# Talking-heads attention with a gated feed-forward on one core: value products in runs of two chunks, loads issued from ScalarE's queue, and a weight repack in three steps

## The chip, the core and the metric

The kernel runs on one core of a Trainium2 chip. Its engines are TensorE (PE in the profile; its weight loads are listed as PEld), VectorE (DVE), ScalarE (ACT), GpSimd (POOL) and SyncE (SP), each with its own stream of instructions that it works off in order, and they meet through semaphores. DMAs are issued here from SP's stream and from ACT's stream; in the profile the issuing instructions stand under SPq and ACTq. The metric is the device time of one execution in microseconds. Less is better.

## What is computed

Four batches, twelve heads, 448 positions and a head size of 64. Scores are mixed across heads before the softmax (`w_pre`) and the probabilities after it (`w_post`); the result, 1792 tokens of 768, goes through a gated feed-forward layer of width 1536. All of it in 32-bit floats.

```python
scores = (q @ k.T) / sqrt(64)                     # per batch and head, 448 x 448
scores = einsum('bhij,hg->bgij', scores, w_pre)   # heads mixed
attn   = exp(scores - max(scores)); attn = attn / (sum(attn) + 1e-9)
attn   = einsum('bhij,hg->bgij', attn, w_post)    # heads mixed again
x      = (attn @ v) as 1792 tokens x 768
out    = (sigmoid(x @ w_gate) * (x @ w_val)) @ w_out
```

The matrices `moe_w_gate`, `moe_w_val` and `moe_w_out` come as 64-bit floats in memory, 36 tiles of 128 x 768, and are narrowed to 32 bits on the chip.

## The kernel before

**Attention (`_attention`).** The queries of a batch are cut in blocks of 120, 120, 120 and 88 rows, sixteen blocks in all, and a block in groups of ten rows: 180 groups. A group is a slot of a software pipeline, and the loop at L434 walks the slots t. For each (block, head) two matmuls (`qk`, L163 and L164) make the scores in PSUM, and a copy (`keep`, L172 on ACT for odd heads, L174 on DVE for even ones) puts them into a staging tile `st`, of which there are two, used by alternate blocks. `regroup` (L198) is a DMA from `st` into a tile `T`, which turns ten rows of twelve heads into 120 partitions; it is issued from SP up to seven slots ahead, into one of five `T` buffers. `premix` (L203) multiplies `T` by `w_pre` into a PSUM tile `pm` (two buffers), `rowmax` (L210, DVE) takes the row maximum, `expo` (L219, ACT) the exponential, `scale` (L233, POOL) and `p_lo` (L248, DVE) split the scaled probabilities in two 16-bit halves `ph` and `pl`, `postmix` (L260, PE, tile `mx`, two buffers) mixes the heads again, and `mix` (L266, ACT) puts the result into one of two block tiles. In the first 13 and the last 16 groups the halves are left out and a 32-bit product is made instead. When a block is whole, `av` (L280) multiplies it by the values: six chunks c per block, each 8 matmuls that the trace counts as 16, spread over the slots in which the next block is worked on; after chunks 3 and 5 ACT copies the sums out (L288) and issues their store (L289).

In a slot of the loop PE is given, in this order, `qk` of a coming block, `premix(t+4)`, `av` if one is due, `postmix(t)`. DVE is given the copy of `qk`, then `rowmax(t+4)`, then the small sums and `p_lo(t+1)`. ACT is given its copy of `qk`, `mix(t-1)`, the jobs of the plan (the `av` copies among them) and `expo(t+4)`.

The inputs are loaded by `k_load` (L122, 18 tiles, four buffers in `raws`), `q_load` (L140, 15 tiles, two buffers) and `v_load` (L181, 12 tiles, three buffers), one load per slot at most, by the times set at L329 to L353; all are issued from SP, in SP's stream between the regroup DMAs.

**The feed-forward (`_Moe`).** Its products are made by a seven-product scheme on 2 x 2 quarters, in two pairs of batches, and every 32-bit operand is split in two parts, `hi` by a cast on ACT (`round`, L875) and `lo` by a subtraction on DVE (`rest`, L878), so that three matmuls stand for one (`gate`, L888, and `out_mm`, L899). Sums and differences of quarters are made on DVE (`tt`, L881), PSUM is copied out by ACT (`copy`, L905) and added up on DVE (`sum`, L908); L911 is the sigmoid and L914 the product with the gate. For the first pair each weight tile k is loaded as raw 64-bit words (`load_raw`, L839, SP, three buffers in `raws`), its upper half is made in place in two steps on ACT (`top`: L848 takes the fifth byte of each 8-byte word, sign-extended, into the word's upper 32 bits, L852 turns the bfloat16 in the word's last two bytes into a float16), `convert` (L857, DVE) merges the two 32-bit words, and `keep_w` (L861) stores the 32-bit tile for the second pair.

Which unit does which of these tasks when is decided before anything is issued, by a planner in Python (`order_tasks`) that goes through the tasks with the prices that each carries (`by_dve`, `by_act`, the `pe` entries) and with the room for tiles of each kind (`ROOM`, `KIND`). It starts some thirty slots before the last group, so the first weight tiles are repacked while attention still runs. `slot`, `between` and `run` then issue the tasks in the planned order. The matmuls of the feed-forward keep one fixed order; what the prices move is the order of the tasks on ACT, DVE and SP.

## Time and profile before

| | us |
|---|---|
| median of 3 runs | 1010.58 |
| lowest and highest | 1008.87, 1017.09 |
| the profiled execution | 1007.51 |
| its span, first to last instruction | 1005.6 |
| attention: up to the first matmul of the feed-forward at | 508.3 |
| the feed-forward's second pair and tail, from about 725 to | 1005.6 |

The profile is of one execution. In its views times count from the start of the span; PE and PEld overlap, since a weight load runs beside the matmul before it. Idle time of an engine is put down to what ended it last, and idle time of an engine that nobody waits for costs nothing. The chain of waits is followed backwards from the last instruction, so its shares say what the time hung on at each moment, and not how much would go if one step went.

### The profile page before, as it was taken

How to read it: one execution, taken by the hardware profiler on the slowest of the kernel's cores; microseconds unless marked ns; L12 is line 12 of the kernel's file. 1: busy time of each engine (PE TensorE's matmuls, PEld its weight loads, DVE VectorE, ACT ScalarE, POOL GpSimd, SP SyncE). 2: the span in 40 equal slices, each digit the busy share in tenths (PEclk: the TensorE clock that was granted, in tenths of full speed). 3: DMA queues.
4: the chain of work that ended last, by engine and by line, in shares of the span. 5: the costliest groups of instructions: out<-in, count | busy, mean ns of one | idle time of the engine just before them, and what ended most of it. 6: DMA issues, size and time to landing. Idle time of an engine off the chain costs nothing.

```text
span 1005.6 us, 17847 instructions
## 1 busy us (share of the span) xinstructions
PE 939.6 (93%) x6606; PEld 749.7 (75%) x6606; DVE 696.9 (69%) x1243; ACT 613.1 (61%) x1061; POOL 275.7 (27%) x354
## 2 busy tenths in 40 slices
PE   7889999899989999979789999999899999999998
PEld 2656676566766677656568888888699999999997
DVE  7556777578665667645468877788988766669882
ACT  3555667566665666667596888799455444446460
POOL 6246755478546864422210000000000000000000
PEclk8899999999999999999999999999899999999999
DMA  5666567665677665766825555778644321210002
GB/s 162 158 165 171 133 129 190 156 169 114 146 195 173 139 125 118 176 164 133 237 90 185 192 189 188 250 242 292 207 146 166 94 63 52 75 48 1 28 10 74
DMA packets 71333, 144.48 MB, mean 144 GB/s; under 512 B 18167, under 2 KB 49999, under 8 KB 71247
## 3 DMA queue, kind: packets, MB, share of 16 engines
q1 hardware_dynamic: 58024, 137.63, 50.0%
q10 hardware_dynamic: 13223, 5.70, 2.1%
q8 instruction: 53, 0.87, 0.3%
q14 instruction: 33, 0.27, 0.1%
HBM read 79.44 MB, written 25.17 MB: 104 GB/s over the span
## 4 chain that ended last, share of the span: by engine, by line
PE 63%; DMA 17%; ACT 11%; DVE 5%; issue 3%; SPq 1%; ACTq 0%; DVEq 0%
PE bank L888 18%; DMA T<-st 13%; PE bank L899 13%; PE pm L203 11%; PE mx L260 9%; PE av L280 6%; DMA raws<-in_w_dram 4%; ACT raws L852 4%; PE qk L163 3%; ACT m_GV L875 3%; PE qk L164 2%; ACT raws L848 2%; ACT m_FWTR L905 1%; DVE st L174 1%; DVE m_FWTR L881 1%
## 5 line engine op out<-in xcount | busy, mean ns | idle before, releaser
L888 PE MATMUL bank<-m_GV 128*128 128x448 f32 x1512 | 314.2, 368 | 10.8 <-ACT m_FWTR L905 5.2
L888 PEld LDWEIGHTS bank<-m_GV 128*128 128x128 f32 x1512 | 284.1, 189 | 40.0 <-ACT m_FWTR L905 7.8
L210 DVE TENSOR_SCALAR_CACHE_REDUCE junk<-pm 128x448 f16<-128x448 f32 x180 | 112.0, 622 | 132.5 <-PE pm L203 129.1
L203 PE MATMUL pm<-T,w 120*128 120x448 f32 x360 | 173.2, 563 | 28.7 <-DMA T<-st 19.8
L219 ACT ACTIVATE e<-pm,nm 128x448 f32<-128x448 f32 x180 | 114.3, 635 | 124.7 <-DVE junk L210 71.9
L878 DVE TENSOR_TENSOR m_GV<-m_FWTR,m_GV 128x768 fp32r<-128x768 f32 (+1 forms) x137 | 154.4, 1138 | 49.9 <-ACT m_GV L875 47.9
L875 ACT CAST m_GV<-m_FWTR 128x768 fp32r<-128x768 f32 (+1 forms) x137 | 134.9, 1001 | 56.7 <-DVE m_FWTR L881 28.3
L899 PE MATMUL bank<-m_GV 128*128 128x448 f32 x756 | 158.9, 371 | 6.5 <-ACT m_GV L875 3.9
L899 PEld LDWEIGHTS bank<-m_GV 128*128 128x128 f32 x756 | 143.8, 191 | 21.2 <-ACT m_GV L875 4.7
L233 POOL TENSOR_SCALAR ph<-e,ss 128x448 f16<-128x448 f32 x151 | 98.5, 660 | 156.4 <-ACT e L219 94.8
L260 PEld LDWEIGHTS <-ph 128*128 128x128 f16 x1208 | 91.6, 98 | 47.4 <-issue 38.7
L248 DVE SCALAR_TENSOR_TENSOR pl<-e,ss,ph 128x448 f16<-128x448 f32 x151 | 122.2, 809 | 4.1 <-POOL ph L233 3.8
L266 ACT ACTIVATE mix<-mx,fm 128x480 f32<-128x480 f32 x180 | 121.2, 673 | 2.5 <-PE mx L260 2.5
L280 PEld LDWEIGHTS av<-mix,v 128*64 128x64 f32 x1504 | 73.6, 138 | 59.1 <-issue 40.5
L260 PE MATMUL mx<-w2hi,pl 128*128 128x120 f16 x604 | 105.2, 217 | 9.5 <-DVE pl L248 9.5
L260 PE MATMUL mx<-w2hi,ph 128*128 128x120 f16 x604 | 106.3, 219 | 1.5 <-POOL qhh L149 0.6
L260 PE MATMUL mx<-w2lo,ph 128*128 128x120 f16 x604 | 105.3, 217 | 0.0
L203 PEld LDWEIGHTS pm<-T,w 120*128 120x128 f32 x360 | 66.4, 194 | 46.7 <-ACT mix L266 15.7
L280 PE MATMUL av<-mix,v 128*64 128x120 f32 (+1 forms) x1504 | 93.5, 268 | 0.0
L905 ACT COPY m_FWTR<-bank 128x448 f32<-128x448 f32 x96 | 52.8, 554 | 60.4 <-PE bank L888 45.4
L163 PE MATMUL qk<-kT,qhh 128*120 128x448 f32 (+1 forms) x180 | 80.1, 445 | 2.4 <-POOL qhh L149 1.9
L174 DVE COPY st<-qk 120x448 f32<-120x448 f32 (+1 forms) x92 | 56.3, 613 | 35.4 <-PE qk L164 14.6
(70 smaller groups left out, 1041.6 us busy)
## 6 DMA issues: line engine op xcount, KB each, us to landing
T<-st SPq DMA_DIRECT2D x180, 210.0 KB
raws<-in_w_dram SPq DMA_DIRECT2D x36, 767.6 KB
w<-m_FWTR SPq DMA_DIRECT2D x36, 384.0 KB
m_FWTR<-w SPq DMA_DIRECT2D x31, 384.0 KB
raws<-in_kd_dram SPq DMA_DIRECT2D x18, 448.0 KB
qd<-in_qd_dram SPq DMA_DIRECT2D x11, 720.0 KB
raws<-w SPq DMA_DIRECT2D x17, 384.0 KB
v<-in_vb_dram SPq DMA_DIRECT2D x12, 512.0 KB
```

The source lines that it names most:

```text
L163: nc.tensor.matmul(sc[:n, :S], lhsT=hh[:, h, :n], rhs=kt, start=True, stop=False)
L203: nc.tensor.matmul(ps[:, :S], lhsT=w1, rhs=t_t.pop(t), start=True, stop=True)
L210: nc.vector.tensor_scalar(junk, sc_t[t][:, :S], -SCALE, None, op0=ALU.mult, op1=ALU.min, accum_out=nm)
L219: nc.scalar.activation(out=e, in_=sc_t.pop(t)[:, :S], func=AF.Exp, bias=nm_t.pop(t), scale=SCALE, accum_out=ss)
L248: nc.vector.scalar_tensor_tensor(pl, e_t.pop(t), ss_t.pop(t), p_t[t][0], op0=ALU.mult, op1=ALU.subtract)
L260: nc.tensor.matmul(ps[:, jb, :], lhsT=a[:, JB[jb]:JB[jb] + 128], rhs=w, start=(i == 0), stop=(i == len(terms) - 1))
L266: nc.scalar.activation(out=mixes[bi % 2][:, :, :, r0:r0 + R], in_=mx_t.pop(t).rearrange("p j (g r) -> p j g r", r=R), func=AF.Copy, scale=fm)
L280: nc.tensor.matmul(av_t[bi][64 * i:64 * i + 64, c % 4, :n], lhsT=vt[b, u][:, h + i, jb, :], rhs=mixes[bi % 2][:, jb, 2 * c + i, :n], start ...
L875: self.nc.scalar.copy(self.f32(hi).bitcast(F32R), self.f32(f))
L878: self.nc.vector.tensor_tensor(self.f32(lo).bitcast(F32R), self.f32(f), self.f32(hi), op=ALU.subtract)
L888: self.nc.tensor.matmul(self.f32(bank), lhsT=w[a][:, k], rhs=x[b][:, k], start=self.START[i] and k == r == 0, stop=k == self.KH - 1 and r ...
L899: self.nc.tensor.matmul(self.f32(bank), lhsT=w[a][:, k], rhs=b[bb], start=self.START[i] and j == k == r == 0, stop=j == OUT_TILES - 1 and ...
```

## The change

Five things are changed.

1. `av` takes its chunks in twos: chunk c is placed at the slot of chunk c - c % 2, and the two follow each other on PE, after `postmix(t)` and not before it (`tail`).
2. In a slot `premix` and `rowmax` now come before `qk` and its copy.
3. `k_load`, `q_load` and `v_load` are issued from ACT's stream, and so is `load_raw` in slots more than seven before the end of attention (four of the 36 tiles); the others stay on SP.
4. `top` has three steps. ACT takes the fifth byte of each word into a dense tile `half` of 768 16-bit numbers, DVE turns these from bfloat16 into float16 in place, and ACT spreads them, as 16-bit integers times 65536, into the upper 32-bit words. There is one `half`, so a tile's third step comes before the next tile's first. `raws` grows from 4608 to 4992 elements, and the last `ROOM` has four tiles of kind T where it had five.
5. The planner's prices: a fixed 0.18 where 0.07 stood for an ACT task, 0.205 where 0.19 stood for a matmul, and 0.4 for the new step on DVE.

```diff
 I32 = mybir.dt.int32
+I16 = mybir.dt.int16
 I8 = mybir.dt.int8
...
         t = kld[len(kraw) % len(kld)]
-        nc.sync.dma_start(out=t, in_=kd[b, c])
+        nc.scalar.dma_start(out=t, in_=kd[b, c])
         kraw[b, c] = t
...
         t = qld.tile([128, H * QB], F32, tag="qd", name="qd")
-        nc.sync.dma_start(out=t[:, :H * n], in_=qd[b, :, H * i0:H * (i0 + n)])
+        nc.scalar.dma_start(out=t[:, :H * n], in_=qd[b, :, H * i0:H * (i0 + n)])
         qraw[bi] = t[:, :H * n].rearrange("p (h s) -> p h s", s=n)
...
         t = vst.tile([128, QUAD, 4, D], F32, tag="v", name="v")
-        nc.sync.dma_start(out=t.rearrange("p h j d -> p (h j d)"), in_=vb[b, u])
+        nc.scalar.dma_start(out=t.rearrange("p h j d -> p (h j d)"), in_=vb[b, u])
         vt[b, u] = t
...
         for c in range(KC):
-            at(spread(c, KC, s0, s1), av, bi, c)
+            at(spread(c - c % 2, KC, s0, s1), av, bi, c)
             if bi == NBK - 1:
...
         todo = plan.get(t, ())
+        if 0 <= t + SOFT < NG:
+            premix(t + SOFT)
+            rowmax(t + SOFT)
         for fn, args in todo:
...
                 fn(*args)
-        if 0 <= t + SOFT < NG:
-            premix(t + SOFT)
-            rowmax(t + SOFT)
         sums = t % 2 == 0 and 0 <= t + PREP < NG + 1
...
             mix(t - 1)
+        tail = (av, moe.between)
         for fn, args in todo:
-            if fn is not qk:
+            if fn is not qk and fn not in tail:
                 fn(*args)
...
             expo(t + SOFT)
+        if t >= NG:
+            for fn, args in todo:
+                if fn in tail:
+                    fn(*args)
         if t == NG:
...
             postmix(t)
+            for fn, args in todo:
+                if fn in tail:
+                    fn(*args)
     return moe
...
     START = (True, True, False, True, False, False, False)
-    KIND = dict(raw="R", early="W", w="W", s="W", t="F", whi="V", wlo="V", q="F", qhi="G", qlo="G", c="T", snap="T", tmp="T")
+    KIND = dict(raw="R", half="H", early="W", w="W", s="W", t="F", whi="V", wlo="V", q="F", qhi="G", qlo="G", c="T", snap="T", tmp="T")
     SLOT = 1.9
-    ROOM = ((-15, dict(F=5, G=4, W=6, V=4)), (-7, dict(G=2, V=2, T=3)), (0, dict(G=3, W=2, V=2)), (9.6, dict(F=4, G=5, W=2, V=0, T=5, R=0)))
-    AHEAD = dict(raw=120.0, early=120.0, w=50.0, s=12.0, t=15.0, whi=12.0, wlo=12.0, q=40.0, qhi=15.0, qlo=15.0, c=40.0, snap=40.0, tmp=40.0)
+    ROOM = ((-15, dict(F=5, G=4, W=6, V=4)), (-7, dict(G=2, V=2, T=3)), (0, dict(G=3, W=2, V=2)), (9.6, dict(F=4, G=5, W=2, V=0, T=4, R=0)))
+    AHEAD = dict(raw=120.0, half=120.0, early=120.0, w=50.0, s=12.0, t=15.0, whi=12.0, wlo=12.0, q=40.0, qhi=15.0, qlo=15.0, c=40.0, snap=40.0, tmp=40.0)
...
         self.copies = dram.tile([len(self.order), 128, self.WE], F32, name="w32")
-        self.free = dict(F=[], G=[], W=[], V=[], T=[], R=[raws[:, i:i + 2 * self.WE] for i in range(0, raws.shape[1], 2 * self.WE)])
+        self.free = dict(F=[], G=[], W=[], V=[], T=[],
+                         R=[raws[:, i:i + 2 * self.WE] for i in range(0, raws.shape[1] - 2 * self.WE + 1, 2 * self.WE)],
+                         H=[raws[:, -self.WE // 2:]])
         self.banks, self.at = {}, {}
...
     def by_act(self, n):
-        return dict(act=0.07 + 0.86e-3 * n)
+        return dict(act=0.18 + 0.86e-3 * n)
...
                 task(self.load_raw, dict(dma=2.2), ((("raw", k), True),), k)
-                for step in range(2):
-                    task(self.top, self.by_act(self.WE), ((("raw", k), True),), k, step)
+                for step in range(3):
+                    task(self.top, dict(dve=0.4) if step == 1 else self.by_act(self.WE),
+                         ((("raw", k), step == 2), (("half", k), step < 2)), k, step)
                 task(self.convert, self.by_dve(self.WE), ((("raw", k), False), (w, True)), w, k)
...
                     uses = [(name, False) for name in ws[n][i] + x[i]] + [(bank, True)]
-                    task(self.gate, dict(pe=0.19 * 3 * KH), uses, bank, ws[n][i], x[i], i, e)
+                    task(self.gate, dict(pe=0.205 * 3 * KH), uses, bank, ws[n][i], x[i], i, e)
                     self.gathered(p, n, i, e)
...
                     uses = [(name, False) for names in [ws[FN + j][i]] + [hs[u][i] for u in x] for name in names]
-                    task(self.out_mm, dict(pe=0.19 * 3 * KT), uses + [(bank, True)], bank, ws[FN + j][i],
+                    task(self.out_mm, dict(pe=0.205 * 3 * KT), uses + [(bank, True)], bank, ws[FN + j][i],
                          [hs[u][i] for u in range(self.FU)], i, j, m)
...
-        self.nc.sync.dma_start(out=self.at["raw", k].bitcast(I8)[:, :8 * self.WE - 3], in_=self.src[k].bitcast(I8)[:, 3:])
+        self.loads.dma_start(out=self.at["raw", k].bitcast(I8)[:, :8 * self.WE - 3], in_=self.src[k].bitcast(I8)[:, 3:])
...
-        raw = self.at["raw", k]
+        raw, half = self.at["raw", k], self.at["half", k]
         if step == 0:
+            self.nc.scalar.activation(out=half.bitcast(I16), in_=raw.bitcast(I8).rearrange("p (e b) -> p e b", b=8)[:, :, 4],
+                                      func=AF.Copy, scale=2.0 ** 8)
+        elif step == 1:
+            self.nc.vector.tensor_copy(half.bitcast(F16), half.bitcast(BF16))
+        else:
             word = raw.bitcast(I32).rearrange("p (e w) -> p e w", w=2)[:, :, 1]
-            self.nc.scalar.activation(out=word, in_=raw.bitcast(I8).rearrange("p (e b) -> p e b", b=8)[:, :, 4],
-                                      func=AF.Copy, scale=2.0 ** 24)
-        else:
-            out, src = (raw.bitcast(dt).rearrange("p (e h) -> p e h", h=4)[:, :, 3] for dt in (F16, BF16))
-            self.nc.scalar.copy(out, src)
+            self.nc.scalar.activation(out=word, in_=half.bitcast(I16), func=AF.Copy, scale=2.0 ** 16)
...
         a = t - self.NG
+        self.loads = self.nc.scalar if a < -7 else self.nc.sync
         if a == self.ROOM[0][0]:
...
     with tc.manual_schedule():
-        raws = top.tile([128, 3 * H * D * 2], F32, name="raws")
+        raws = top.tile([128, 13 * H * D // 2], F32, name="raws")
         with ExitStack() as c2:
```

How the instructions stand before and after is shown at three places. The first is PE in slots 164 and 165, near the end of attention, where `postmix` is the short 32-bit form (`mx<-w2s,e`); `pm` is `premix`, `av` the value products, x8 one chunk. Before:

```order
L203 MATMUL pm<-T,w_121 128x448
L280 MATMUL av<-mix_132,v 64x120 x8
L260 MATMUL mx<-w2s,e 128x120 x4
L203 MATMUL pm<-T,w_121 128x448
L260 MATMUL mx<-w2s,e 128x120 x4
```

And in the changed kernel, from the same slot on:

```order
L204 MATMUL pm<-T,w_121 128x448
L261 MATMUL mx<-w2s,e 128x120 x4
L281 MATMUL av<-mix_132,v 64x120 x16
L204 MATMUL pm<-T,w_121 128x448
L261 MATMUL mx<-w2s,e 128x120 x4
```

Two chunks stand in one run, behind `mx`, where one chunk stood between `pm` and `mx` in every second slot.

The second place is DVE in two slots of the last third of attention: `st<-qk` is the copy of the scores, `junk,nm<-pm` is `rowmax`, `pl` is `p_lo`, and the two `ss` rows are the small sums. Before:

```order
L174 COPY st<-qk 88x448
L210 TENSOR_SCALAR junk,nm<-pm 128x448
L224 TENSOR_SCALAR ss<-ss 128x2
L248 SCALAR_TENSOR_TENSOR pl<-e,ss,ph 128x448
L227 RECIPROCAL ss<-ss 128x2
L210 TENSOR_SCALAR junk,nm<-pm 128x448
L248 SCALAR_TENSOR_TENSOR pl<-e,ss,ph 128x448
```

And in the changed kernel:

```order
L211 TENSOR_SCALAR junk,nm<-pm 128x448
L175 COPY st<-qk 88x448
L225 TENSOR_SCALAR ss<-ss 128x2
L249 SCALAR_TENSOR_TENSOR pl<-e,ss,ph 128x448
L228 RECIPROCAL ss<-ss 128x2
L211 TENSOR_SCALAR junk,nm<-pm 128x448
L249 SCALAR_TENSOR_TENSOR pl<-e,ss,ph 128x448
```

The copy into `st` has changed places with the row maximum of the same slot.

The third place is ACT where the feed-forward begins, just after the first sigmoid has loaded its table. `m_GV<-m_FWTR` are the casts of `round`, `mix` is the last of attention's output on its way to memory (`xs`), `raws` are the steps of `top`. Before:

```order
L875 CAST m_GV<-m_FWTR 128x768 x2
L848 ACTIVATE raws<-raws 128x768
L852 CAST raws<-raws 128x768
L288 COPY mix_131<-av 128x4x88
L289 DMA xs<-mix_131 128x4x88
L848 ACTIVATE raws<-raws 128x768
L288 COPY mix_131<-mx 128x2x88
L289 DMA xs<-mix_131 128x2x88
L852 CAST raws<-raws 128x768
L905 COPY m_FWTR<-bank_7008 128x448
L875 CAST m_GV<-m_FWTR 128x768
```

And in the changed kernel:

```order
L888 CAST m_GV<-m_FWTR 128x768 x2
L289 COPY mix_131<-av 128x4x88
L290 DMA xs<-mix_131 128x4x88
L289 COPY mix_131<-mx 128x2x88
L290 DMA xs<-mix_131 128x2x88
L888 CAST m_GV<-m_FWTR 128x1344
L918 COPY m_FWTR<-bank_7011 128x448
L888 CAST m_GV<-m_FWTR 128x768
```

The four steps of two weight tiles that stood before the last cast are gone from this stretch; their like comes later on ACT, behind ten casts and copies more.

## Rows read from the trace of the kernel before

**Rows 1.** The page of the profile: the first part, busy time, share of the span and number of instructions of each engine, and from the second part the granted clock of PE in 40 equal slices, in tenths of full speed.

```profile
PE 939.6 (93%) x6606; PEld 749.7 (75%) x6606; DVE 696.9 (69%) x1243; ACT 613.1 (61%) x1061; POOL 275.7 (27%) x354
...
PEclk8899999999999999999999999999899999999999
```

**Rows 2.** Busy time of each engine in nine stretches: the stretch and its length, then PE, PEld, DVE, ACT and POOL, each busy us and (x instructions), then PE's granted clock, the DMA engines' mean busy share, and GB/s.

```profile
25.00:500.00 475.00, 436.88 (x4106) 303.93 (x4106) 299.83 (x785) 294.61 (x660) 254.98 (x333) 0.98 0.67 156
45.00:70.00 25.00, 19.03 (x124) 12.87 (x123) 12.11 (x37) 13.68 (x32) 8.75 (x14) 1.00 0.72 183
100.00:157.00 57.00, 56.01 (x569) 40.15 (x566) 40.97 (x101) 36.96 (x84) 37.14 (x47) 1.00 0.61 130
226.00:248.00 22.00, 21.63 (x204) 15.22 (x205) 17.79 (x39) 14.82 (x35) 18.20 (x23) 1.00 0.60 118
440.00:470.00 30.00, 29.13 (x292) 20.30 (x287) 17.83 (x55) 23.94 (x49) 8.62 (x14) 1.00 0.60 123
...
525.00:700.00 175.00, 168.43 (x808) 152.26 (x808) 137.17 (x169) 145.05 (x170) 0.00 (x0) 0.99 0.63 215
675.00:700.00 25.00, 24.73 (x123) 22.62 (x121) 20.02 (x22) 23.93 (x25) 0.00 (x0) 1.00 0.90 300
700.00:725.00 25.00, 18.76 (x71) 15.42 (x72) 24.64 (x26) 13.20 (x15) 0.00 (x0) 0.86 0.59 193
725.00:1006.00 281.00, 276.87 (x1352) 253.41 (x1351) 202.81 (x227) 129.57 (x175) 0.00 (x0) 1.00 0.22 73
```

**Rows 3.** The chain of waits, the part from 160 to 180 us in order of time: start, length, and what it hung on. First two slots in which PE sets the pace, the first with a value chunk of 88 columns, then two waits for a regroup DMA, each counted from the DMA's issue.

```profile
161.69 0.75 PE pm L203 x2
162.44 0.76 PE av L280 x16
163.20 0.74 PE mx L260 x12
...
164.39 0.75 PE pm L203 x2
165.14 0.63 PE mx L260 x12
...
168.62 8.26 DMA T<-st
...
178.70 8.95 DMA T<-st
```

**Rows 4.** The instructions of PE in order of time at the end of attention, where the last block's six chunks of 88 columns stand in one run: start, length with the drain of the last one, line, and x instructions (x64 is four chunks).

```profile
512.18 2.65 PE L280 MATMUL av<-mix,v 128*64 128x88 f32 x64
514.66 1.38 PE L280 MATMUL mx<-mix,v 128*64 128x88 f32 x32
```

**Rows 5.** What SP issued between 44 and 61 us, in order of time: start, how long the issue held SP, line, and the tile that is filled.

```profile
44.37 2.53 SPq L198 DMA_DIRECT2D T<-st  x1
46.95 0.60 SPq L181 DMA_DIRECT2D v<-in_vb_dram  x1
47.65 2.79 SPq L198 DMA_DIRECT2D T<-st  x1
...
58.44 2.75 SPq L181 DMA_DIRECT2D v<-in_vb_dram  x1
```

**Rows 6.** The issues of line 198 (the regroup DMA) in 45 to 70 us: least, median and greatest ns that one held SP, first and last start.

```profile
L198 SPq DMA_DIRECT2D T<-st x9: 769/2530/2985, 44.4 to 66.9; - x9
```

**Rows 7.** The same line in 226 to 248 us.

```profile
L198 SPq DMA_DIRECT2D T<-st x8: 769/868/1940, 226.0 to 243.2; - x8
```

**Rows 8.** What PE waited for up to 525 us, the two largest: who waited for whom, us in total, times, longest.

```profile
PE pm L203 <- DMA T<-st: 19.8, 18, 2.4
PE mx L260 <- DVE pl L248: 9.5, 6, 3.5
```

**Rows 9.** All engines' waits in 426 to 438 us, where the longest of these falls.

```profile
DVE st L174 <- DMA T<-st: 6.7, 1, 6.7
ACT e L219 <- DVE ss L224: 6.4, 1, 6.4
...
PE mx L260 <- DVE pl L248: 3.5, 1, 3.5
```

**Rows 10.** Instructions in order of time at the start of the feed-forward, ACT's steps of `top` and the matmul that waits: start, length, line, operation; in brackets the idle time before and what ended it.

```profile
515.90 0.92 ACT L848 ACTIVATE raws<-raws 128x768 int32<-128x768 int8 x1
...
516.85 1.99 ACT L852 CAST raws<-raws 128x768 f16<-128x768 bf16 x1
...
519.57 0.91 ACT L848 ACTIVATE raws<-raws 128x768 int32<-128x768 int8 x1 [0.44 <-ACT mix L288]
...
521.10 1.95 ACT L852 CAST raws<-raws 128x768 f16<-128x768 bf16 x1 [0.44 <-ACT mix L288]
...
524.20 0.67 PE L888 MATMUL bank<-m_GV 128*128 128x448 f32 x2 [4.31 <-ACT m_GV L875]
```

**Rows 11.** Groups of ACT's instructions from 525 to 725 us by line: shapes, count, busy us, mean ns of one, idle before.

```profile
L852 ACT CAST raws<-raws 128x768 f16<-128x768 bf16 x29 | 58.3, 2011 | 0.2
...
L848 ACT ACTIVATE raws<-raws 128x768 int32<-128x768 int8 x29 | 28.0, 965 | 8.7 <-DMA raws<-in_w_dram 8.7
```

**Rows 12.** Two groups of DVE's instructions over the whole span, with the same columns: the merge of a weight tile, and a reciprocal of two numbers per partition.

```profile
L857 DVE SCALAR_TENSOR_TENSOR m_FWTR<-raws 128x768 int32<-128x768 int32 x36 | 34.0, 953 | 14.4 <-ACT raws L852 14.3
...
L227 DVE RECIPROCAL ss<-ss 128x2 f32<-128x2 f32 x90 | 14.2, 157 | 0.5
```

## The prediction

> **What bounds the kernel now.** I read the page first, then the windows, the chain and the waits of each stretch. The page gives PE 93% of the span and a clock below full only at the start and in one slice just after 700 us [rows 1], so whatever goes must come out of PE's 65 idle us or out of its dear instructions. The windows say where these lie [rows 2]. From 25 to 500 us, 180 slots in about 475 us (2.64 us a slot), PE is idle for 38 us. The idleness is uneven: four stretches (the first 100 to 157 us, the last 440 to 470 us, with 225 to 272 and 345 to 395 between them, together 184 of the 475 us, 39%) have PE 97 to 98% busy, while 45 to 70 us has 19.03 of 25. From 525 to 725 us PE loses 6.6 + 6.2 us beside ACT (23.93 of 25 just before 700) and DVE (24.64 of 25 just after), and a clock of 0.86 there costs more on top. After 725 us it is 276.87 of 281: a second pair that only fewer or shorter matmuls could shorten.
>
> In attention the chain shows two kinds of slot: `pm`, `av`, `mx` end to end, and slots that hang on a regroup DMA which lands 8 to 9 us after its issue [rows 3]. The waits name the same: PE waits 19.8 us for `T`, 18 times, and 9.5 us for `pl` [rows 8].
>
> **A. Values in runs of two.** A chunk alone costs its own 0.76 us and makes the `mx` behind it 0.74 instead of 0.63; `pm` ahead is 0.75 either way. That is 0.87 us a visit [rows 3]. In a run, four chunks of the same 88 columns take the 2.48 us between the two starts, 0.62 each [rows 4]. So a visit avoided is worth 0.25 us. Fifteen blocks (the sixteenth's chunks run together already) save three visits each: 45 × 0.25 = 11.3 us where PE sets the pace throughout. It does so in 39% of attention; elsewhere a shorter `av` lengthens a wait for `T`. That would be 4.4 us; as the other parts make those waits shorter I take −6. Bounds: −11, and +6 if the changed neighbours (`pm` then `qk`, `mx` then `av`, `av` then `pm`), which no row shows, cost in each of the 180 slots a third of the 0.25 us that an avoided visit is worth (180 × 0.09 less some 10). Two chunks together also mean one slot that is longer by 0.62 us and one that is shorter, which two `mx` buffers and a four-slot lead of `expo` cover.
>
> **B. Loads off SP's queue.** Where loads are due, an issue of the regroup DMA holds SP for 2.5 to 2.8 us, and a value load 0.6 or 2.75 [rows 5]; the median is 2.53 us in 45 to 70 us [rows 6] and 0.87 us in 226 to 248, where no load comes [rows 7], and PE is 21.63 of 22 there [rows 2]. With 2.64 us a slot, an SP that needs 2.5 us for a `T` and up to 2.75 for a load in the same slot falls behind, and its seven slots of lead are used up. Taking 45 loads and four raw tiles away removes SP's part. It doesn't remove the bytes: the DMA engines are 72% busy in the burst against 60% without [rows 2], and the `T`s there wait on that too. The bounds are nothing, and all of the 19.8 us; I take −4, a fifth of it, since a landing 8 to 9 us after the issue [rows 3] uses up most of the 13 us (five slots) that five `T` buffers allow, whoever issues the loads.
>
> The Trainium skill speaks against this part: "DMA: Bandwidth & Descriptors", section "Issuing engines are not separate DMA queues", says that DMAs of any engine end up on the same 16 engines, and that another issuer saves only the sequencer's time. By it alone B is 0. The row of 2.53 against 0.87 us agrees in that the issue holds SP longer when the engines are fuller; it doesn't say which way the cause runs.
>
> On ACT the loads are new. In attention ACT is busy 294.61 of 475 us [rows 2], so it has 1.0 us idle in a slot of 2.64, and an issue of a store leaves 0.44 us idle on it [rows 10]. At 0.44 to 0.6 us a load is hidden in that. Each load also waits for its buffer; behind it on ACT stand `expo`, the odd `st` copies and `mix`, for which POOL, DVE and PE's `pm` and `postmix` wait. By the times of the plan a buffer has been read some slots before it is filled again, so I put that at 0; at 2.75 us a load it is the rival on the other side, below. The first query load on ACT lies in the first 25 us, which DVE's splits pace: 0 to +2.
>
> **D. `rowmax` ahead of the copy.** Around 427 us DVE stood 6.7 us in an `st` copy, because a late regroup was still reading that tile; `rowmax` stood behind it, so ACT waited 6.4 us for sums and PE 3.5 us for `pl` [rows 9]. In the new order `rowmax` is done first and the four-slot lead is kept. Over attention PE's waits of this kind are 9.5 us [rows 8]. Not all of them go, for `pm` will wait for its `T` soon after the copy does, and the odd heads' copies on ACT still stand ahead of `expo`. I take −4; bounds −9.5 and +3 (an `st` copy later by one 0.6-us `rowmax`, with `regroup` behind it, where SP has no lead).
>
> **C. Tops.** Both old steps together are 2.011 + 0.965 = 2.98 us of ACT a tile, 29 tiles after 525 us [rows 11]. The fifth-byte step stays near 0.965; the spread of a dense 16-bit tile into 32-bit words writes the same strided words as that old step did from a worse source, so 0.95 again; the cast that wrote every fourth half-word goes to DVE, dense. ACT saves 1.05 × 29 = 30 of its 158 us between 525 and 725. DVE gains 31 casts, each between 0.157 us (a two-number operation) and 0.953 (a whole tile's merge) [rows 12]; I take 0.4, for 768 elements need several times the small one and these are half words without a second source: 12.4 us on DVE's 161.8 of that stretch, 174. PE's least there is 879 matmul rows at 276.87/1352 = 0.205 us, 180 us. So ACT, dear from 675 to 700, drops away, and DVE becomes as near a bound as ACT was; of the 20 us over PE's least I give back about a quarter, −5.5. At the start of the feed-forward PE waits 4.31 us for a cast that has 0.92 + 1.99 + 0.91 + 1.95 us of tops ahead of it on ACT [rows 10]; the order has moved them behind it, and I take −2.5, as attention's last copies remain. C is −8. Bounds: −20 (all of the loss) and +12 (every cast of DVE on PE's path).
>
> **The rest.** One tile of kind T fewer and the planner's prices: 0, since after 725 us PE is 276.87 of 281 in a fixed order; at worst +4, that idleness doubled.
>
> **The sum.** −6 − 4 − 4 − 8 = −22 against the profiled execution's 1007.5 (span 1005.6 and 1.9 around it): 985.5. The median of the runs is 3.1 us above that execution, so 988.6, put at 989.
>
> **Rivals.** All on the median's scale, 1010.6.
>
> R1, the queue changes nothing: the regroups are slow because the DMA engines are full, not because SP is. For it: landings at 8 to 9 us from issue. Against: with the engines 60% busy the issues take 0.87 us and PE is 98% busy. A −4, B 0, D −2, C −8: 996.6. This is also what the skill's section named above makes of the change.
>
> R2, lock-step through the single `half`: ACT's next fifth-byte step waits for the third step of the tile before, and that for DVE's cast, which stands behind 0.95-us merges and longer work. ACT then loses one DVE operation, 0.95 to 1.5 us, per tile and saves nothing. For it: DVE is 24.64 of 25 after 700 us. Against: the planner puts other ACT work between. C = +2 instead of −8: 998.6.
>
> R3, SP's queue was nearly all of it. With SP free the bursts run like 226 to 248 us and PE sets the pace throughout, so A counts more too: −9 − 19.8 − 7 − 8 = −44, 966.8.
>
> R4, slower: loads hold ACT. If an issue on ACT behind full DMA rings holds it as long as the worst on SP, 2.75 us [rows 5], each of 49 loads overruns ACT's 1.0 us of slack by 1.75 us, 86 us; the loads come in some 13 runs of following slots, and each run first uses up one slot of lead, 13 × 2.64 = 34. The rest, +52, delays `expo` and so PE; with A, D and C as forecast 1044.6. It turns the result from a mean hold of some 2.1 us on (49 × 1.1 − 34 = 20 against −18). For it: the 2.53 medians. Against: the v load of 0.60 in the same burst, and the 2.75 that lies right behind `T`s on SP, which no load on ACT does.
>
> R5, the third step is as dear as the old cast (2.0 us, strided writes): ACT saves nothing and DVE pays, C = +4: 1000.6.
>
> **Chances.** Forecast 0.42, R1 0.15, R2 0.15, R3 0.14, R5 0.06, R4 0.08. The range is 964 to 1007: it takes in R1, R2, R5 and most of R3, and leaves out R4, the far half of R3's spread and the upper ends of R1 and R2, about 0.2. A change of 1% (10 us) is about what a measurement of this kernel can tell from none. Faster than 1000.5: 0.40 from the forecast, 0.14 from R3, 0.10 from R1, 0.09 from R2, 0.03 from R5, 0.76. Slower than 1020.7: R4 less a little, 0.07. Within 1%: 0.17.
>
> **What would show it.** A: on PE `av` in 45 pairs, near 1.24 + 0.11 us for 88 columns, and PE's busy time before 525 us down by about 11 us. B: the median regroup issue in 45 to 70 us below 1.5 us and PE's wait for `T` below 15 us; with 2.5 us still there, R1 holds. R4 would show as idle time of ACT behind its own load issues and PE waiting for `pl` or `e`. D: no wait of several us of DVE's `st` copy with `rowmax` behind it, and PE's wait for `pl` under 5 us. C: first and third step near 0.95, the cast near 0.4, no wait of 4 us at the first matmuls of the feed-forward, and PE's loss over its 180 us between 525 and 725 under 15 us; ACT waiting for the cast on DVE, tile after tile, would be R2. I am wrong altogether if PE's busy time in attention rises, for then the new order of its instructions has a price that the rows of before don't show.

## The result, and the profile after

The changed kernel takes 978.70 us (median of 4 runs, 977.59 to 979.46), the kernel before 1013.19 us in the same comparison (1008.87 to 1017.09): a ratio of 0.966, with a 95% interval of 0.9612 to 0.9707. The profiled executions differ by 29.0 us of span, 1005.6 against 976.6; the one of before lies below its median.

First the page of the profile after, with the shares of the chain by engine in its last line:

```profile
PE 925.5 (95%) x6606; PEld 749.5 (77%) x6606; DVE 719.6 (74%) x1279; ACT 575.6 (59%) x1061; POOL 277.8 (28%) x354
...
PEclk8999999999999999998999999998899999999999
...
PE 65%; DVE 6%; DMA 5%; issue 1%; ACT 1%; SPq 1%; POOL 0%; ACTq 0%; POOLq 0%; DVEq 0%
```

The same last line of the page before:

```profile
PE 63%; DMA 17%; ACT 11%; DVE 5%; issue 3%; SPq 1%; ACTq 0%; DVEq 0%
```

The two lines can't be set side by side as they are: the shares of after add up to 79%, because its chain could be followed back only to 191.6 us, where group 69 begins. From that group to the end in both kernels, DMA has 116 us of the chain before and 49 after, ACT 109 and 12, PE 510 and 638. So most of what hung on DMA and ACT hangs on PE now; how much each of them gave, the chain doesn't say. The PE row answers to [rows 1]; its busy time fell by 14 us with the same 6606 matmuls.

Where the 29 us came from, by the start of the same piece of work in the two traces (the row maximum of a group, and the matmuls of the feed-forward by their share of 2268):

| | before | after | gained by then |
|---|---|---|---|
| row maximum of group 20 | 74.5 | 68.2 | 6.3 |
| of group 80 | 232.9 | 220.5 | 12.4 |
| of group 150 | 412.7 | 393.6 | 19.1 |
| first matmul of the feed-forward | 508.3 | 487.3 | 21.0 |
| 5% of them | 542.0 | 515.6 | 26.4 |
| 35% | 688.8 | 657.5 | 31.3 |
| 40% | 722.8 | 695.4 | 27.4 |
| end | 1005.6 | 976.6 | 29.0 |

Attention gave 21 us, the first matmuls of the feed-forward 5.4, the repack 4.9, of which 3.9 were lost again at its end.

Busy time by stretch in the kernel after, with the columns of [rows 2]:

```profile
45.00:70.00 25.00, 23.84 (x176) 17.46 (x174) 16.88 (x46) 17.21 (x40) 13.12 (x20) 1.00 0.73 209
75.00:440.00 365.00, 349.44 (x3556) 245.20 (x3554) 266.15 (x659) 231.94 (x544) 226.82 (x286) 1.00 0.65 157
440.00:487.00 47.00, 38.19 (x309) 30.47 (x308) 21.59 (x50) 26.51 (x53) 11.34 (x14) 0.89 0.70 193
500.00:675.00 175.00, 170.09 (x823) 153.66 (x821) 153.63 (x209) 129.16 (x177) 0.00 (x0) 1.00 0.63 220
675.00:697.00 22.00, 16.34 (x51) 13.43 (x52) 21.22 (x21) 9.10 (x11) 0.00 (x0) 0.69 0.67 231
697.00:977.00 280.00, 275.83 (x1354) 253.83 (x1353) 200.12 (x224) 129.01 (x176) 0.00 (x0) 1.00 0.21 69
```

In 45 to 70 us PE is 23.84 of 25 busy where it was 19.03, with the DMA engines at 73% where they were at 72%: as many busy engines, and 5 us of waiting less. From 500 us on ACT is no longer full (129.16 of 175 us), and DVE is nearly: 153.63 of 175, and 21.22 of 22 at the end of the repack.

The issues of the regroup DMA in 45 to 70 us of the kernel after, with the columns of [rows 6]:

```profile
L199 SPq DMA_DIRECT2D T<-st x11: 768/777/1663, 44.8 to 69.2; - x11
```

The median fell from 2530 to 777 ns. What PE still waits for in the kernel after up to 500 us, as in [rows 8]:

```profile
PE pm L204 <- DMA T<-st: 15.4, 10, 4.5
PE pm L204 <- ACT e L220: 9.9, 12, 1.5
PE mx L261 <- DVE pl L249: 3.5, 5, 1.9
```

The wait for `pl` is down from 9.5 us; the one for `T` only from 19.8 to 15.4, and half of what is left lies behind 440 us, where the feed-forward's first transfers run. The wait for `e` (the exponential, on ACT) has grown; in the kernel before, up to 525 us, it was

```profile
PE pm L203 <- ACT e L219: 3.8, 3, 1.9
```

Of the 9.9 us now, 9.0 (11 of the 12 waits) come behind a load that ACT issued at most 3.5 us ahead of that exponential. This is a price of part B.

The steps of the new `top` in the kernel after, 500 to 697 us, with the columns of [rows 11], first on ACT:

```profile
L865 ACT ACTIVATE raws<-raws 128x768 int32<-128x768 int16 x32 | 29.0, 907 | 2.7 <-DVE raws L862 2.5
L859 ACT ACTIVATE raws<-raws 128x768 int16<-128x768 int8 x31 | 28.4, 916 | 0.8 <-DMA raws<-in_w_dram 0.4
```

and on DVE:

```profile
L862 DVE CAST raws<-raws 128x768 f16<-128x768 bf16 x32 | 11.3, 354 | 0.7 <-ACT raws L859 0.5
```

0.907 and 0.916 us stand where 2.011 and 0.965 stood, and ACT waits 2.5 us in all for DVE's cast.

### The profile page after: what moved, and what is told of

Its sections match the earlier page's. It is cut to its first block, busy times and chain, and to the rows that moved or that the text cites. A ratio compares the mean times of both kernels' runs of the same rounds, so it can differ in the third digit from the quotient of the medians.

```text
span 976.6 us, 17919 instructions
## 1 busy us (share of the span) xinstructions
PE 925.5 (95%) x6606; PEld 749.5 (77%) x6606; DVE 719.6 (74%) x1279; ACT 575.6 (59%) x1061; POOL 277.8 (28%) x354
## 4 chain that ended last, share of the span: by engine, by line
PE 65%; DVE 6%; DMA 5%; issue 1%; ACT 1%; SPq 1%; POOL 0%; ACTq 0%; POOLq 0%; DVEq 0%
PE bank L901 29%; PE bank L912 14%; PE pm L204 8%; PE mx L261 6%; DMA T<-st 5%; PE av L281 4%; DVE m_GV L891 2%; PE qk L164 2%; PE qk L165 2%; DVE m_FWTR L894 1%; DVE m_FWTR L921 1%; DVE junk L211 0%; DVE pl L249 0%; SPq L885 0%; DVE m_FWTR L870 0%
## 5 line engine op out<-in xcount | busy, mean ns | idle before, releaser
L204 PE MATMUL pm<-T,w 120*128 120x448 f32 x360 | 180.9, 584 | 25.7 <-DMA T<-st 15.4
L249 DVE SCALAR_TENSOR_TENSOR pl<-e,ss,ph 128x448 f16<-128x448 f32 x151 | 128.7, 852 | 11.3 <-POOL ph L234 11.2
L164 PE MATMUL qk<-kT,qhh 128*120 128x448 f32 (+1 forms) x180 | 125.3, 696 | 0.4 <-DVE st L175 0.4
L261 PEld LDWEIGHTS <-ph 128*128 128x128 f16 x1208 | 85.6, 98 | 36.3 <-issue 27.1
L173 ACT COPY st<-qk 120x448 f32<-120x448 f32 (+1 forms) x92 | 48.8, 530 | 92.1 <-PE qk L165 86.3
L204 PEld LDWEIGHTS pm<-T,w 120*128 120x128 f32 x360 | 55.0, 192 | 37.3 <-ACT e L220 16.6
L281 PE MATMUL av<-mix,v 128*64 128x120 f32 (+1 forms) x1504 | 83.0, 264 | 0.0
L921 DVE TENSOR_TENSOR m_FWTR<-bank,m_FWTR 128x448 f32<-128x448 f32 x90 | 55.9, 622 | 36.0 <-PE bank L912 20.9
```

The source lines that it names most:

```text
L164: nc.tensor.matmul(sc[:n, :S], lhsT=hh[:, h, :n], rhs=kt, start=True, stop=False)
L204: nc.tensor.matmul(ps[:, :S], lhsT=w1, rhs=t_t.pop(t), start=True, stop=True)
L249: nc.vector.scalar_tensor_tensor(pl, e_t.pop(t), ss_t.pop(t), p_t[t][0], op0=ALU.mult, op1=ALU.subtract)
L261: nc.tensor.matmul(ps[:, jb, :], lhsT=a[:, JB[jb]:JB[jb] + 128], rhs=w, start=(i == 0), stop=(i == len(terms) - 1))
L281: nc.tensor.matmul(av_t[bi][64 * i:64 * i + 64, c % 4, :n], lhsT=vt[b, u][:, h + i, jb, :], rhs=mixes[bi % 2][:, jb, 2 * c + i, :n], start ...
```

## The experiments

Eight runs take the change apart by the four parts that the prediction names A to D: each part alone in the kernel before, and the changed kernel without each part. Four more ask for the mechanism. Ratios are to the kernel before, measured beside each run (medians 1010.63 to 1010.98); the changed kernel's own is 0.966, so differences from it of a few us say nothing.

**A alone, and the rest without A.**

```diff
-            at(spread(c, KC, s0, s1), av, bi, c)
+            at(spread(c - c % 2, KC, s0, s1), av, bi, c)
...
+            if fn is not qk and fn not in tail:
...
             postmix(t)
+            for fn, args in todo:
+                if fn in tail:
+                    fn(*args)
```

Expected of A alone: 

> The kernel before with the value chunks in twos, behind postmix, and nothing else. Theory (parts add, each by its own mechanism): a pair of chunks costs PE 1.93 us more than a slot without one, against 2 x 1.07 for two single visits, 45 pairs x 0.22 = 10 us of PE, of which the waits for T (untouched, some 18 us) swallow half: start of the feed-forward 4 to 8 us earlier, time 4 to 8 us less. Rival (the parts work only together, since a shorter av only lengthens the wait for T): less than 3 us. The regroup issues in 45 to 70 us stay at 2.5 us under both.

Expected without A: 

> The changed kernel with the value chunks one by one again, between premix and postmix. If the parts add, 4 to 10 us slower than the changed kernel (983 to 989); nearer 10 than in the kernel before, as T comes in time and PE sets the pace in most slots. Rival (parts overlap): under 3 us.

A alone: 1011.67 us, ratio 1.0007 (0.9989 to 1.0025). Without A: 979.07 us, 0.9685 (0.9654 to 0.9716). A is worth nothing in either company. On PE it does what was priced. The chain of the kernel after has runs of two chunks, 120 and 88 columns wide:

```profile
250.85 1.79 PE av L281 x32
258.38 1.36 PE av L281 x32
```

From the starts of PE's instructions, an undisturbed slot without `av` takes 1.864 us (`pm` 0.463, `qk` 0.761, `mx` 0.640), one with a pair of 120 columns 3.795 (0.508 + 0.761 + 0.734 + 1.791); with single chunks it is 2.926. So a pair costs 1.93 us and two visits 2 × 1.06 = 2.12, and 0.19 us are saved; at 88 columns it is 0.24. But by the slots' real lengths (start of `pm` to the next, mean between 75 and 440 us) the slots behind give it back:

| | slot with `av` | first behind | second | third | all slots |
|---|---|---|---|---|---|
| changed, without A | 2.93 | 2.06 | | | 2.527 |
| changed | 3.76 | 1.97 | 2.15 | 2.10 | 2.528 |

Something other than PE holds the mean at 2.53.

**B alone, and the rest without B.**

```diff
-        nc.sync.dma_start(out=t, in_=kd[b, c])
+        nc.scalar.dma_start(out=t, in_=kd[b, c])
...
+        self.loads = self.nc.scalar if a < -7 else self.nc.sync
```

(and the same for `q_load` and `v_load`; `load_raw` goes by `self.loads`.) Expected of B alone: 

> The kernel before with k, q, v and four raw loads issued from ACT, and nothing else. Theory: SP is held by issues in the bursts; the median regroup issue in 45 to 70 us falls from 2.53 to under 1.0 us, PE is over 23 of 25 us busy there, group 20 is reached 5 to 6 us earlier, and the time is 6 to 12 us less. Rival R1 (the DMA engines are full, whoever issues): the issue time may fall, but the regroups land as late as before, PE's wait for T stays near 18 us, and the time moves less than 3 us. Rival R4's mechanism would show as idle time of ACT behind its loads and a slower kernel.

Expected without B: 

> The changed kernel with all loads on SP again. Theory: regroup issues of 2.5 us are back in 45 to 70 us, PE is near 19 to 21 of 25 us busy there, 6 to 12 us slower than the changed kernel (985 to 991). Rival R1: within 3 us of it.

B alone: 985.18 us, ratio 0.9743 (0.9718 to 0.9768), 25 us less. Without B: 1001.27 us, 0.9902 (0.9864 to 0.9940), 22.6 us more than the changed kernel. B is most of the result, and both runs lie beyond what was expected. The regroup issues in 45 to 70 us with B alone:

```profile
L198 SPq DMA_DIRECT2D T<-st x11: 768/769/3107, 43.2 to 69.7; - x11
```

PE's waits with B alone, the three largest; the second and third name the same tiles as [rows 8]:

```profile
PE pm L203 <- ACT e L219: 10.1, 8, 4.2
PE pm L203 <- DMA T<-st: 5.8, 4, 2.2
PE mx L260 <- DVE pl L248: 4.5, 2, 4.3
```

19.8 and 9.5 us have become 5.8 and 4.5. PE's idle time up to the feed-forward fell from 45.0 to 30.4 us, and its busy time by 7.2 us at the same mean granted clock, 0.97; why the busy time fell was not followed up. A regroup lands no sooner after its issue than before (median over all 180: 7.11 us, 6.96 before). It is issued sooner: 11.06 us ahead of its `premix` in the median, 9.88 before. From 43 to 70 us issues held SP for 94% of the time before and 45% with B alone. That rules out R1. R4 comes about only in part: its sign is there, the wait for `e` that grew from 3.8 to 10.1 us, but the 49 loads hold ACT for 0.81 us on average in the kernel after (0.60 with B alone), against the mean of 2.1 us from which it would have decided. The dearest of them are the key loads:

```profile
L123 ACTq DMA_DIRECT2D raws<-in_kd_dram x18: 334/1328/2596, 35.9 to 303.3; - x18
```

**D alone, and the rest without D.**

```diff
+        if 0 <= t + SOFT < NG:
+            premix(t + SOFT)
+            rowmax(t + SOFT)
         for fn, args in todo:
             if fn is qk:
                 fn(*args)
-        if 0 <= t + SOFT < NG:
-            premix(t + SOFT)
-            rowmax(t + SOFT)
```

Expected of D alone: 

> The kernel before with premix and rowmax ahead of qk and its copy, and nothing else. Theory: a DVE or ACT that stands in an st copy no longer holds the row maximum; PE's wait for pl falls from 9.5 to under 4 us, time 3 to 6 us less. Rival (the wait only moves to the next slot, where pm wants a T that comes late from the later copy): PE's wait for T grows by what the wait for pl loses, time within 2 us, or longer.

Expected without D: 

> The changed kernel with qk and its copy ahead of premix and rowmax again. Theory: the waits for pl come back (over 6 us), 3 to 6 us slower than the changed kernel. Rival (with loads off SP the st copies are hardly late, and the order is worth nothing): within 2 us.

D alone: 1008.77 us, 0.9975 (0.9957 to 0.9993). Without D: 980.21 us, 0.9703 (0.9671 to 0.9735), which isn't told apart from the whole. PE's waits with D alone:

```profile
PE pm L203 <- DMA T<-st: 23.5, 25, 3.1
PE mx L260 <- DVE pl L248: 8.2, 5, 3.2
```

The wait for `pl` lost 1.3 us and the one for `T` gained 3.7, as the rival had it. The long wait for `pl` [rows 9] was a late regroup seen through DVE. Fewer late regroups make it rarer: with B alone the waits for `pl` are 2 where they were 6. One of these two is the same chain again, near 411 us: DVE stands 5.5 us in the copy and PE 4.3 us for `pl`. In the changed kernel DVE still stands 4.2 us there and PE 1.9; without D it is 7.5 and 1.0, so that D shortened PE's part of it isn't shown.

**C alone, and the rest without C.**

```diff
-            word = ... self.nc.scalar.activation(out=word, in_=raw...[:, :, 4], func=AF.Copy, scale=2.0 ** 24)
-            self.nc.scalar.copy(out, src)
+            self.nc.scalar.activation(out=half.bitcast(I16), in_=raw...[:, :, 4], func=AF.Copy, scale=2.0 ** 8)
+            self.nc.vector.tensor_copy(half.bitcast(F16), half.bitcast(BF16))
+            self.nc.scalar.activation(out=word, in_=half.bitcast(I16), func=AF.Copy, scale=2.0 ** 16)
```

(with `ROOM`, `raws` and the planner's prices as in the change.) Expected of C alone: 

> The kernel before with the three-step tops, four tiles of kind T, and the planner's new prices, and nothing else. Theory: attention's end is not moved by over 2 us (start of the feed-forward near 507), the wait of 4.3 us at its first matmuls is gone, and from the first feed-forward matmul to the end 7 to 9 us less (497 before, 489 after with the whole change): time 7 to 9 us less. Rival (part of that gain belongs to the order of the tail, which lets av and the feed-forward's pieces follow postmix): less than 4 us.

Expected without C: 

> The changed kernel with the two-step tops, five tiles of kind T and the old prices. Theory: start of the feed-forward near 487 as in the changed kernel, the wait at its first matmuls back, from its first matmul to the end about 497 us against 489: 7 to 9 us slower (986 to 988). Rival: under 4 us, the rest being the tail's order.

C alone: 1000.58 us, 0.9898 (0.9871 to 0.9924). Without C: 986.11 us, 0.9760 (0.9726 to 0.9794), 7.4 us more than the whole. From the first feed-forward matmul to the end it is 497.3 us before and 490.7 with C alone, 497.1 without C and 489.3 in the whole: 7 to 8 us by either pair.

**Bytes or instructions on SP.** The kernel before with part B, but each load's first 16 bytes per partition stay on SP.

```diff
-        nc.sync.dma_start(out=t, in_=kd[b, c])
+        for eng, cut in ((nc.sync, slice(0, 4)), (nc.scalar, slice(4, None))):
+            eng.dma_start(out=t.rearrange(...)[:, cut], in_=kd[b, c].rearrange(...)[:, cut])
```

Expected: 

> The kernel before with the loads on ACT as in the run with that part alone, but the first four elements of each partition of every k, q and v load still issued from SP, at the same place in SP's stream and behind the same wait for the buffer; ACT issues the rest. So SP keeps 45 instructions, their waits and as many descriptors, and loses only the bytes. Theory Q (bytes ahead of the regroups in SP's queue hold up the regroups' issue): about as fast as with the loads wholly on ACT, 985 to 990, median regroup issue in 45 to 70 us under 1.2 us. Theory S (SP's stream: the time of the issuing instruction and its wait for a free buffer): 1000 or more.

Measured: 1018.04 us, ratio 1.0075 (1.0042 to 1.0108). All that B gave is gone, with next to none of the loads' bytes on SP. But the time alone doesn't tell bytes from instructions, for ACT is held in this kernel as it is in neither of the two it is compared with. PE's two largest waits up to 525 us:

```profile
PE pm L206 <- ACT e L222: 28.9, 12, 5.9
PE pm L206 <- DMA T<-st: 9.6, 7, 3.3
```

The wait for `T` is half of what it was before, and the one for `e` is new. In the trace the DMAs of both queues share eight semaphores, and an issue waits until the DMA that last used its own has landed. With 45 more DMAs ACT stands idle for 30 us in all before its loads (2.8 with B alone); near 176 us, for example, it waits 4.5 us until a 16-byte piece that SP issued 8 us earlier has landed. So bytes and instructions have to be told apart by SP's issues themselves. SP's issues in this kernel, in order of time, with the columns of [rows 5]:

```profile
46.70 2.66 SPq L201 DMA_DIRECT2D T<-st  x1
49.41 0.49 SPq L184 DMA_DIRECT2D v<-in_vb_dram  x1
49.99 2.91 SPq L201 DMA_DIRECT2D T<-st  x1
52.95 0.49 SPq L123 DMA_DIRECT2D raws<-in_kd_dram  x1
53.54 2.67 SPq L201 DMA_DIRECT2D T<-st  x1
```

A 16-byte load costs SP its own 0.49 us, and the regroup behind it takes 2.7 to 2.9 us, as behind a whole load. SP issues without a gap of 0.1 us, so no wait for a buffer is in this; from 43 to 70 us issues hold it for 95% of the time, as in the kernel before. Sorted by what SP issued just before, from 25 to 465 us: a regroup behind a regroup held SP for 1.41 us on average in the kernel before (121 of them, median 1.05), one behind a k, q or v load 2.28 (43 of them), and here 1.33 and 2.29. Part of that difference goes with the pauses between issues: of the regroups issued without one (under 0.15 us), those behind a regroup took 1.68 us and those behind a load 2.36, here 1.69 and 2.39. A load's own issue is 1.06 us on average in both kernels. So the size of the load makes no difference to SP; having an instruction there does. Why a regroup's issue is longer behind it stays open, and so does how much of B's 25 us the SP stream is worth by itself.

**What holds the slot at 2.53 us.** The changed kernel with half the regroup's bytes, with and without A. From the sixth group on the other half of each `T` holds old scores, so these two kernels compute something else and serve only to time the transfers.

```diff
+    Ts = []
...
-        T = tp.tile([KR, S], F32, tag="T", name="T")
-        nc.sync.dma_start(out=T, in_=st_t[bi][r0:r0 + R])
+        if t < 5:
+            Ts.append(tp.tile([KR, S], F32, tag=f"T{t}", name="T"))
+        T, n = Ts[t % 5], S if t < 5 else S // 2
+        nc.sync.dma_start(out=T[:, :n], in_=st_t[bi][r0:r0 + R, :, :n])
```

Expected with A: 

> The changed kernel with five fixed T tiles, of which from the sixth group on the regroup fills only the first 224 of 448 columns, so the regroups move half the bytes; the rest of T holds old scores. Everything else works on full tiles. Theory F (once the loads are off SP's queue the regroup transfers themselves set the pace in the slots without a value product): 8 us or more faster than the changed kernel, slots of 2.53 us on average fall below 2.45. Rival G (these slots are paced by ACT, DVE and POOL and by the depth of the buffers): within 4 us of the changed kernel.

Expected without A: 

> The same half regroups, with the value chunks one by one again. Under F the 10 us of PE that the pairs save come out here: 4 to 10 us slower than with pairs and half regroups. Under G the pairs are still worth nothing: within 3 us of it.

With A 950.66 us, ratio 0.9393 (0.9359 to 0.9426), 28 us below the changed kernel; without A 956.87 us, 0.9460 (0.9429 to 0.9491). The stretch from 75 to 440 us with A:

```profile
75.00:440.00 365.00, 362.75 (x3692) 257.48 (x3690) 274.84 (x685) 242.44 (x568) 231.90 (x292) 1.00 0.51 124
```

and without:

```profile
75.00:440.00 365.00, 365.00 (x3679) 253.40 (x3677) 262.97 (x680) 240.98 (x563) 232.51 (x290) 1.00 0.50 123
```

PE is busy throughout, a slot takes 2.41 and 2.42 us, and a regroup lands after 3.6 us instead of 7.1. So theory F holds: in the changed kernel the regroup transfers set the pace of attention. By which way isn't separated: with half the bytes a regroup also holds SP for 0.78 us on average instead of 1.44, a key load holds ACT for 0.47 instead of 1.35, and of PE's 9.9 us of waits for `e` none over 0.15 us is left. A was expected to be worth 4 to 10 us then, and the times differ by 6.2; but the place is wrong. Group 150's row maximum begins at 382.2 us with A and 382.8 without; the rest arises in the last ten groups. Even on a full PE the pairs gain almost nothing in the steady state: the three slots behind one take 1.90, 1.90 and 1.93 us where a slot behind a single chunk takes 1.87, which gives back 0.12 of the 0.19 us. What the last ten groups owe to A was not followed up.

**The cast on POOL.**

```diff
-            self.nc.vector.tensor_copy(half.bitcast(F16), half.bitcast(BF16))
+            self.nc.gpsimd.tensor_copy(half.bitcast(F16), half.bitcast(BF16))
```

Expected: 

> The changed kernel with the 36 half-word casts on POOL, which is idle after 500 us, instead of DVE. DVE loses 36 x 0.354 us = 12.7 us, and it is 9.5 to 10 of 10 us busy in 660 to 690 us, where PE loses 8 us. Theory: 3 to 7 us faster than the changed kernel (972 to 976). Rival: POOL takes over 1 us for the cast, and through the single half tile ACT waits for it, tile after tile (up to 0.7 us x 32 = 22 us of ACT, which has slack of some 60): same or up to 5 us slower.

Measured: 985.68 us, ratio 0.9739 (0.9694 to 0.9784), 7 us more than the changed kernel, though the intervals of the two ratios overlap a little. The cast on POOL and PE's longest wait in 487 to 720 us:

```profile
L862 POOL CAST raws<-raws 128x768 f16<-128x768 bf16 x31 | 35.5, 1145 | 150.7 <-ACT raws L859 150.7
```

```profile
PE bank L912 <- ACT m_GV L888: 8.5, 2, 7.4
```

1.145 us instead of 0.354, 0.8 us more between the two ACT steps of a tile. ACT waits 5.0 us in all for the cast from 500 us on, where it waited 2.5 for DVE's, far less than the 22 us that the rival allowed. The wait at the end of the repack is 7.4 us where it was 4.35, and from the first feed-forward matmul to the end it is 493.8 us, 4.5 more. The feed-forward also starts 5 us later (492.4 us), and why isn't shown: from 440 us to there POOL has a single cast, and PE waits 9.7 us for `T` there instead of 7.4. What DVE would gain by 12.7 us less work, without a dearer cast, this run doesn't tell. No version ran faster than the changed kernel with the whole of its work.

## Why the prediction was right, and which steps failed

The time lies in the range and 10 us below the forecast, but the sum came out near for the wrong reasons: two terms were mis-sized in opposite directions.

**B is the step that failed: −4 was forecast, −25 alone and −22.6 in company were measured.** R3, priced at 19.8 us for this part, came nearest, and even it was low, since some of the waits for `pl` were late regroups too; it also took A to count more, and A gave nothing. The fifth that the forecast took was reasoned from landings of 8 to 9 us, which leave only 4 of the 13 us that five buffers allow. Those were two pieces of the chain, and the median of all 180 was 6.96 us; and the argument is a reason for B to count, since a slot in which SP falls that far behind is a slot in which PE waits. Beside it stood the sentence in the Trainium skill, "DMA: Bandwidth & Descriptors", section "Issuing engines are not separate DMA queues", that another issuer saves sequencer time alone, usually little beside the DMA itself. The runs agree that the landing stays (6.96 and 7.11 us); but taking 0 from it, as R1 did, was wrong: what left SP's stream was worth 25 us. The rows of before could have shown it: 43 loads of 1.06 us each, and 0.68 us more on the regroup behind each than behind a regroup without a pause, are some 75 us on the stream that PE was waiting for. The price on ACT, put at 0, was not 0: PE's waits for `e` grew by 6 us.

**A: −6 forecast, nothing measured, alone or in company.** The price was right: an avoided visit saves PE 0.24 us at 88 columns and 0.19 at 120, where 0.25 was taken. What failed is the step from PE to the end, the share of 39% in which that saving was to count. In the changed kernel the slots behind a pair give it back to waits, and the regroups set the pace. In the kernel before, A alone was to be worth 4.4 us by that share and gave nothing: while the waits for `T` went down, those for `pl` grew from 9.5 to 13.9 us. Why nothing came of it even in the stretches where PE is 97% busy and more was not followed up.

**D: −4 forecast, −2 alone and none to be told apart in company.** The wait existed, but D alone left 8.2 of its 9.5 us and moved more than that to `T`; fewer late regroups, by B, left 4.5.

**C: −8 forecast, −10 alone and −7.4 in company.** The prices were 0.95, 0.95 and 0.4 us, measured 0.916, 0.907 and 0.354. The split was off: the wait at the start of the feed-forward went wholly (5.4 us where I took 2.5), and the repack returned less, for DVE became full, as the working said. PE in the kernel after, at the end of the repack (in brackets the idle time before, and its releaser):

```profile
667.64 4.69 PE L912 MATMUL bank<-m_GV 128*128 128x448 f32 x22
676.68 1.12 PE L912 MATMUL bank<-m_GV 128*128 128x448 f32 x2 [4.35 <-ACT m_GV L888]
679.02 5.47 PE L912 MATMUL bank<-m_GV 128*128 128x448 f32 x16 [1.23 <-DVE m_GV L891]
686.37 0.80 PE L912 MATMUL bank<-m_GV 128*128 128x448 f32 x2 [1.88 <-ACT m_GV L888]
```

The 3.9 us lost again lie between 35% and 40% of the matmuls. Of 37.9 us there PE is idle for 8.3 (6.5 of 34.0 before). The rest is the clock: from 676.5 to 683.3 and from 686.8 to 693.6 us, at the end of the first of these waits and just after the third, it is granted at its lower level (1.2 GHz), 13.6 us in all where it was 6.8 before, and a matmul takes 0.57 us there instead of 0.37.

R2 (lock-step through `half`) cost 2.5 us of ACT in all and didn't show; R5 fell with the 0.907. The parts alone add up to 0 − 25 − 2 − 10 = −37 us; the whole is −34.5, with an interval from −30 to −39, so no overlap can be told.

Of the signs that the working named, the regroup's issue (0.78 us), the prices of C and the waits for `pl` (3.5 us) came out; PE's wait for `T` (15.4 us, not under 15) and its loss in the repack (18 us of 197 from 500 us on, not under 15) did not, and the sign of R4 was there in part. Two small misreadings of its rows bear on no term: PE was idle for 66 us, not 65, and one of the four busy stretches had PE 99% busy.

## What to carry to other kernels

Before pricing a move between issuing queues, sort the issues of the stream that the bottleneck waits for by what stood before each, those without a pause by themselves: the cost of a foreign DMA there is its own issue plus what the next one takes longer. Then look for the same price on the stream that the DMA moves to. A saving on one engine is worth nothing while another pace-maker, here the transfers, sets the mean over a few slots; halve that one first to see whether the saving exists. A wait on one engine for another can be the same late transfer seen twice, so it shouldn't be counted as a term of its own. And before a probe's time is read, its waits have to be: an added DMA can hold an engine that the question left out.

## What the runs showed that was not expected

A DMA of 16 bytes per partition slows SP's stream as much as a whole load of 3.5 KB or more (1.06 us on average, and 2.3 us for the regroup behind it, in both kernels). The regroups, not PE, bound attention after the change: halving their bytes takes 28 us. Their queue (q1, SP's) and that of the loads and stores (q10, ACT's) from 75 to 440 us of the kernel after, as packets, MB, and share of 16 engines' time:

```profile
q1 hardware_dynamic: 18926, 31.31, 41.8%
q10 hardware_dynamic: 15544, 25.43, 22.5%
```

In the trace's semaphore events a regroup's completion comes in 11 steps and a load's in 16. The Trainium skill ("DMA: Bandwidth & Descriptors", section "Why a DMA increments its semaphore by 16 and not by 1") has the transfer use the largest number of engines up to 16 that divides both outer sizes, 10 for 120 and 10 rows, which agrees: ten steps and one for the six that have no part. An estimate from that rule and the two rows: 0.418 × 16/10 + 0.225 = 0.89 of those ten engines' time, where the row of that stretch shows 0.65 of all sixteen's. That these ten are the limit isn't shown. A regroup that spreads over more engines was not tried.
